# Storing the partial sums of a GLU two rows at a time, with transfer prices and ranks of the order fitted anew

## The chip, the cores and the metric

The kernel runs on one core of one Trainium2 chip. The metric is the time of one execution on the device in microseconds; lower is better. Engines are named as in the profile: PE (TensorE matmul), PEld (its weight load), DVE (VectorE), ACT (ScalarE), POOL (GpSimd) and SP (SyncE, which here only issues transfers).

## The reference

Two branches work on the same input and are mixed row by row. A is a state-space convolution along the sequence, done with Fourier transforms; B is a bilinear GLU without a nonlinearity. A gate of one number per row mixes them.

```python
x = A_u                                                # 1 x 2048 x 512, float32
g = _sigmoid((x * gate_w).sum(-1, keepdims=True))
a = _A_ref(x, log_A_real, A_imag, C_real, C_imag, log_dt, D_skip)   # irfft(rfft(u) * rfft(K)) + u * D_skip
b = einsum((einsum(x, w_gate) * einsum(x, w_up)), w_down)           # F = 1792
return g * a + (1 - g) * b
```

The kernel K of the convolution is itself computed, from 128 complex exponentials for each of 512 channels.

## The kernel before

**GLU.** The 1792 hidden columns are cut into 14 pieces f of 128, in four groups of 3, 3, 4 and 4 (`GROUPS`). The 2048 rows are cut into four column blocks ci of 512, each of four output rows r of 128 partitions, so that an output row t = 4 ci + r is one 128x512 tile, 256 KB. For each group gi and block ci, `hidden(f)` multiplies x by w_gate and w_up into the two PSUM banks pg and pu (one of each), ACT copies pg to h, DVE multiplies pu by h, and h is split into a high part hh (ACT) and a low part hl (DVE). `down` then multiplies by w_down into y (two PSUM banks). Every product is made of three matmuls of 128x512 in fp32r, from the high and low parts of both operands (whi and wlo, xs, dhi and dlo, hh and hl): low times high, high times low, high times high.

**The sums.** `evacuate` (line 722) takes a finished y: ACT scales it by the negated gate into a tile acc, and the tile leaves for the output in memory. In the first group SP stores it; in the others POOL adds it to what is there (`accum_op=ALU.add`). The last block of the last group (`LAST` = 0) is the exception: its four rows stay on the chip and are finished by `ends`, which loads the sums so far and stores the final rows. There are three acc tiles of one row, so the fourth row of a block needs the landing of the first one's transfer.

**Convolution.** Its tables are computed by DVE and ACT for 16 channel blocks, each followed by a matmul step `k_block`; after every fourth come the transforms (`k_first`, `m_second`, `m_inverse`, `m_last`). All their matmuls write tiles named k. They lie between the GLU's matmuls on PE. Intermediate results travel through memory (su_d, sk_d, y_d), and the final pieces are added to the output by POOL.

**The start.** `first_loads` fetches the first x in four pieces of 256 KB (SP) and the first weights w0 in four pieces of 128 KB (the first by ACT's queue, the rest by SP's); `first_split` cuts a piece into high (ACT) and low (DVE), and the first f starts as the pieces come.

**What sets the order.** The program lists all tasks with their engine, an assumed duration, a rank and, for transfers, an assumed size `dma`. `Work.plan` plays the run through with these figures, one task at a time: the one that can start first, ties by rank and place in the list. The order it finds on each engine is what is written out; every engine works strictly in that order. So a changed figure changes the order of the whole run, though not the work. Its figures for transfers: `Bus` serves SP's and POOL's queues side by side with the weights `WEIGHT`; `SENT` and `LANDED` are delays before and behind a transfer; `SURE` is how much later than the planned landing a task that needs the data is placed; `FETCH` and `BEHIND` describe the loading of PE's instructions; `ROOM` says how far an ordinary task may delay an urgent one (h, hh, hl); `EASE` shifts single kinds of tasks by a slack, a rank or a place in the list:

```python
t.slack, t.rank, t.late = t.slack + slack, t.rank + rank, t.late + late
...
if d.dma and d.start > 20.0 and task.engine in self.SURE:
    return d.end + self.SURE[task.engine]
...
for d, end in bus.add(t, start + self.SENT[t.engine], t.dma / self.DMA_RATE / 1000):
    d.end = end + self.LANDED[d.engine]
```

A transfer of figure 256 thus takes 256 / 0.33 / 1000 = 0.78 us in the plan. Instructions are recorded under one line of a helper (L124), so the profile's groups are told apart by the names of the tiles.

## Time and profile before

| | |
|---|---|
| median of three runs | 581.37 us (581.23 to 582.0) |
| the profiled execution's own time | 581.93 us |
| its span, first to last instruction | 580.1 us |
| PE busy | 573.5 us, 99% |
| DVE, ACT, POOL busy | 510.9, 401.6, 113.5 us |
| DMA packets, bytes | 71687, 136.28 MB |

A busy time is the union of an engine's instructions. In the list of groups, a row gives the operation, out<-in with the shapes, the count, busy us, mean ns of one, and the idle time before them with what ended it. In the list of transfers a row gives the issuing queue, the count, KB of each and the median time from issue to landing. The chain of waits follows the run back from its last instruction.

### The profile page before, as it was taken

What the parts mean: (1) busy time and instruction counts of PE and PEld (TensorE: products, weight loads), DVE (VectorE), ACT (ScalarE), POOL (GpSimd) and SP (SyncE); (2) the same over time, 40 slices, a digit from 0 to 9 for tenths busy, and PEclk for the clock granted to TensorE, in tenths of its full rate; (3) what the DMA queues carried; (4) which work ended last, traced back from release to release, by engine and by line L of the source; (5) the groups of instructions that cost most, each with busy time, mean ns of one, the idle gap of its engine ahead of it and who ended that gap; (6) DMA issues with size and microseconds to landing.
All of it is one profiled execution on the core that took longest, in us unless ns stands there. A gap on an engine that the chain in (4) does not pass through costs nothing.

```text
span 580.1 us, 14843 instructions
## 1 busy us (share of the span) xinstructions
PE 573.5 (99%) x5998; PEld 433.8 (75%) x5998; DVE 510.9 (88%) x812; ACT 401.6 (69%) x891; POOL 113.5 (20%) x159
## 2 busy tenths in 40 slices
PE   9999999999999999999999999999999999999997
PEld 6777776888886877788677878876868786776775
DVE  6999999999998999999999999997999996347655
ACT  5459888898588589967896775799877544343351
POOL 0003222311111150321132401102333103111011
PEclk9999999999999999999999999999999999999999
DMA  8999959998655797998779757978989439798986
GB/s 284 403 354 358 395 216 354 269 231 232 140 173 128 281 228 173 261 216 273 201 226 250 188 135 238 213 198 206 292 147 292 72 134 289 246 293 222 291 166 128
DMA packets 71687, 136.28 MB, mean 235 GB/s; under 512 B 6852, under 2 KB 35780, under 8 KB 69188
## 3 DMA queue, kind: packets, MB, share of 16 engines
q1 hardware_dynamic: 47668, 87.10, 43.7%
q0 software_dynamic: 23392, 47.98, 39.6%
q8 instruction: 47, 0.77, 0.6%
q10 hardware_dynamic: 560, 0.26, 0.2%
q14 instruction: 20, 0.16, 0.1%
HBM read 80.27 MB, written 55.05 MB: 233 GB/s over the span
## 4 chain that ended last, share of the span: by engine, by line
PE 97%; DMA 1%; ACT 1%; DVE 1%; issue 0%; DVEq 0%; ACTq 0%
PE pg L124 27%; PE y L124 27%; PE pu L124 27%; PE k L124 16%; DMA y<-in_xT 1%; ACT h L124 0%; DVE y L124 0%; ACT acc L124 0%; ACT xs L124 0%; DVE hl L124 0%; DVE dlo L124 0%; DVE kt L124 0%; DVEq L1568 0%; ACT whi L124 0%; DVE h L124 0%
## 5 line engine op out<-in xcount | busy, mean ns | idle before, releaser
L124 PE MATMUL pg<-xs,whi 128*128 128x512 f32 x448 | 138.9, 391 | 0.4 <-ACT whi L124 0.4
L124 PE MATMUL pu<-xs,whi 128*128 128x512 f32 x448 | 138.2, 390 | 0.0
L124 PEld LDWEIGHTS pg<-xs,whi 128*128 128x128 f32 x448 | 84.3, 188 | 17.7 <-ACT whi L124 0.6
L124 PEld LDWEIGHTS pu<-xs,whi 128*128 128x128 f32 x448 | 84.1, 188 | 17.0
L124 PE MATMUL y<-dhi,hl 128*128 128x512 f32 x224 | 90.2, 403 | 0.7 <-DVE hl L124 0.6
L124 PE MATMUL pg<-xs,wlo 128*128 128x512 f32 x224 | 89.9, 401 | 0.8 <-ACT h L124 0.7
L124 PE MATMUL pu<-xs,wlo 128*128 128x512 f32 x224 | 89.3, 399 | 0.0
L124 PE MATMUL y<-dlo,hh 128*128 128x512 f32 x224 | 87.6, 391 | 0.0
L124 PE MATMUL y<-dhi,hh 128*128 128x512 f32 x224 | 87.1, 389 | 0.0
L124 POOL DMA_DIRECT2D out<-acc x44 | 38.5, 930 | 171.6 <-ACT acc L124 171.0
L124 ACT COPY ev<-k 128x512 f32<-128x512 f32 x112 | 59.3, 597 | 15.8 <-PE k L124 13.3
L124 ACT CAST hh<-h 128x512 fp32r<-128x512 f32 x56 | 34.7, 620 | 41.7 <-DVE h L124 41.3
L124 DVE TENSOR_TENSOR h<-pu,h 128x512 f32<-128x512 f32 x56 | 38.6, 689 | 26.3 <-PE pu L124 23.9
L124 ACT ACTIVATE acc<-y,ngate 128x512 f32<-128x512 f32 x62 | 42.0, 689 | 24.3 <-PE y L124 23.2
L124 PEld LDWEIGHTS pg<-xs,wlo 128*128 128x128 f32 x224 | 42.1, 188 | 21.5 <-issue 10.1
L124 PEld LDWEIGHTS y<-dhi,hl 128*128 128x128 f32 x224 | 42.0, 187 | 21.6 <-issue 8.3
L124 ACT COPY h<-pg 128x512 f32<-128x512 f32 x56 | 33.0, 590 | 32.4 <-PE pg L124 28.6
L124 PEld LDWEIGHTS pu<-xs,wlo 128*128 128x128 f32 x224 | 42.0, 188 | 16.7 <-issue 7.0
L124 PEld LDWEIGHTS y<-dhi,hh 128*128 128x128 f32 x224 | 42.1, 188 | 9.0
L124 PEld LDWEIGHTS y<-dlo,hh 128*128 128x128 f32 x224 | 42.1, 188 | 8.1 <-issue 0.3
L124 DVE TENSOR_TENSOR hl<-h,hh 128x512 fp32r<-128x512 f32 x56 | 38.4, 686 | 3.6 <-ACT hh L124 3.1
L124 DVE TENSOR_TENSOR v<-m,v 128x896 f32<-128x896 f32 x32 | 34.0, 1084 | 0.2
(130 smaller groups left out, 959.1 us busy)
## 6 DMA issues: line engine op xcount, KB each, us to landing
xs<-xs_d SPq DMA_DIRECT2D x36, 512.0 KB, 5.8
out<-acc POOLq DMA_DIRECT2D x44, 256.0 KB, 6.4
raw<-in_wts SPq DMA_DIRECT2D x33, 256.0 KB, 4.9
xs_d<-xs SPq DMA_DIRECT2D x16, 512.0 KB, 6.8
su_d<-ev POOLq DMA_DIRECT2D x32, 256.0 KB, 6.1
y_d<-ts SPq DMA_DIRECT2D x28, 256.0 KB, 6.1
in<-su_d POOLq DMA_DIRECT2D x12, 512.0 KB, 8.0
sk_d<-ev SPq DMA_DIRECT2D x6, 1024.0 KB, 3.9
```

Of the source, the lines that this page charges most:

```text
L124: got = getattr(self.engine, name)(*args, **kw)
```

## The change

1. **Sums in pairs.** A tile acc holds two rows, `[P, 2, D]`, and there are two such tiles instead of three of one row. ACT fills the halves as the two y come; the transfer of both rows starts after the second, with one run of 4 KB for each partition instead of two of 2 KB. There are 8 stores by SP and 22 additions by POOL where there were 16 and 44. The two rows that `ends` takes over lie in the halves of one tile.
2. **A shared buffer.** The convolution's small products and squares (tile `sq`) use the buffer `m` of the large ones.
3. **The first tile.** The first quarter of x comes in two halves of 64 partitions, by SP's and by ACT's queue; the first piece of w0 follows on ACT's queue. The weights of f = 0 are laid out on the host so that each of the four pieces is one run of 1 KB per partition instead of two of 512 B; `product` and `first_split` index them accordingly. The high part of w0's first piece is cast by DVE instead of ACT.
4. **Figures.** The sizes `dma` of most transfers, and `WEIGHT`, `SENT`, `LANDED`, `SURE`, `FETCH`, `BEHIND`, `ROOM`, are set anew, and so is the table `EASE`.

```diff
+PAIR = 620
 class Bus:
-    WEIGHT = 1.0, 1.58
+    WEIGHT = 1.0, 1.24
...
-    BLOCK, FIRST, LEAD, FETCH = 256, 193, 64, 5.0
+    BLOCK, FIRST, LEAD, FETCH = 256, 193, 64, 5.5
-    ROOM = {"dve": 0.6, "act": 0.4}
+    ROOM = {"dve": 0.7, "act": 0.4}
-    BEHIND = 1.3
+    BEHIND = 1.05
     EASE = {
-        "act:k/e:0.4": (3, 0, 0),
+        "act::0.21": (1, 0, 0),
+        "act:k/ev:0.59": (0.0, -1, 0),
+        "act:k/x:0.32": (0.0, -1, 0),
+        "act:k/x:0.59": (0.5, 0, 0),
...
-        "act:t/rt:0.77": (0.0, 0, -200),
-        "act:ts/xs:0.62": (0.0, 2, 0),
-        "dve:ev/y:0.6": (3, 0, 0),
-        "dve:in/whi/wlo:0.69": (0.0, 1, 0),
-        "dve:k/in:0.42": (3, 0, 0),
+        "act:ri/v:1.46": (0.5, 0, 0),
+        "act:v/sq:1.17": (0.0, 0, 20),
+        "act:y/acc:0.69": (0.0, 0, 60),
+        "dve:in/whi/wlo:0.69": (0.0, 1, -200),
+        "dve:k/kt:0.42": (0.0, -1, 0),
...
-        "pe:kt/k/ri/e:2.13": (0.0, 0, -200),
+        "dve:m/v:1.09": (0.0, 0, -20),
+        "dve:v/x:0.4278": (0.0, 0, -200),
+        "sp:in:0.42": (0.0, 1, 0),
+        "sp:raw:0.42": (3, 0, 0),
-    SENT = {"sp": 1.15, "act": 1.15, "pool": 1.98}
-    LANDED = {"sp": 1.79, "act": 1.79, "pool": 1.5}
-    SURE = {"pe": 3, "act": 2, "dve": 2}
+    SENT = {"sp": 1.35, "act": 1.35, "pool": 1.86}
+    LANDED = {"sp": 1.56, "act": 1.56, "pool": 1.62}
+    SURE = {"pe": 3, "act": 1.5, "dve": 1.5}
...
-        add("sp", 0.42, lambda: sp.dma_start(t.t, src), w=[t], dma=256, rank=rank)
+        add("sp", 0.42, lambda: sp.dma_start(t.t, src), w=[t], dma=305, rank=rank)
...
-        add("pool", 0.95, lambda: pool_q.dma_start(lo.t, src, accum_op=ALU.add), w=[lo], dma=485 * n if n > 1 else 414, rank=0)
+        add("pool", 0.95, lambda: pool_q.dma_start(lo.t, src, accum_op=ALU.add), w=[lo], dma=416 * n if n > 1 else 361, rank=0)
...
-            add("sp", 0.42, lambda t=t, k=k, kt=kt: sp.dma_start(t.t[:, k], xsrc(kt)), w=[(t, k)], dma=256, rank=-1)
             e, q = ("sp", sp) if kt else ("act", act)
-            add(e, 0.42, lambda q=q, ks=ks: q.dma_start(w0.t[:, :, ks], wsrc[:, :, ks]), w=[(w0, ("k", kt))], dma=128, rank=-1)
+            cuts = (slice(0, P // 2), slice(P // 2, P)) if kt == 0 else (slice(0, P),)
+            for n, cut in enumerate(cuts):
+                ex, qx = ("act", act) if n else ("sp", sp)
+                add(
+                    ex, 0.42, lambda t=t, k=k, kt=kt, cut=cut, qx=qx: qx.dma_start(t.t[cut, k], xsrc(kt)[cut]),
+                    w=[(t, (k, n)) if len(cuts) > 1 else (t, k)], dma=256 // len(cuts), rank=-1,
+                )
+            add(e, 0.42, lambda q=q, ks=ks: q.dma_start(flat[:, ks], wts[0][:, ks]), w=[(w0, ("k", kt))], dma=128, rank=-1)
...
-        add("act", 0.38, lambda: act.copy(cut(hi.t), src()), r=[(t, k)], w=[(hi, k)], rank=0)
+        if kt:
+            add("act", 0.38, lambda: act.copy(cut(hi.t), src()), r=[(t, k)], w=[(hi, k)], rank=0)
+        else:
+            add("dve", 0.35, lambda: dve.tensor_copy(cut(hi.t), src()), r=[(t, k)], w=[(hi, k)], rank=0)
...
-    def product(pg, which, w, x, kt, after, first):
-        base = which * D + kt * P
+    def product(pg, f, which, x, kt, after, first):
+        w = ws[f]
+        base = which * D + kt * P if f else 2 * kt * P + which * P
...
     def evacuate(gi, ci, r, y):
-        t = 4 * ci + r
+        t, k = 4 * ci + r, r % 2
...
-        acc = new("glu", "acc", [P, D], bufs=3)
+        if not k:
+            sums["acc"] = new("glu", "acc", [P, 2, D], bufs=2)
+        acc = sums["acc"]
         add(
-            "act", 0.69, lambda: act.activation(acc.t, y.t, AF.Copy, scale=ngate[:, t : t + 1]),
-            r=[y, (m_gate, ci)], w=[acc], rank=0,
+            "act", 0.69, lambda: act.activation(acc.t[:, k], y.t, AF.Copy, scale=ngate[:, t : t + 1]),
+            r=[y, (m_gate, ci)], w=[(acc, k)], rank=0,
         )
         if final:
-            ending.append((r, acc))
+            ending.append((r, lambda: acc.t[:, k], (acc, k)))
+        elif not k:
+            return
         elif gi == 0:
-            add("sp", 0.42, lambda: sp.dma_start(ov[:, t, :], acc.t), r=[acc], w=[(m_out, t)], dma=134)
+            add(
+                "sp", 0.42, lambda: sp.dma_start(ov[:, t - 1 : t + 1, :], acc.t), r=[acc],
+                w=[(m_out, t - 1), (m_out, t)], dma=392,
+            )
         else:
             add(
-                "pool", 0.95, lambda: pool_q.dma_start(ov[:, t, :], acc.t, accum_op=ALU.add),
-                r=[acc, (m_out, t)], dma=431, rows=[t],
+                "pool", 0.95, lambda: pool_q.dma_start(ov[:, t - 1 : t + 1, :], acc.t, accum_op=ALU.add),
+                r=[acc, (m_out, t - 1), (m_out, t)], dma=PAIR, rows=[t - 1, t],
             )
...
-        q = new("tab", "sq", [P, 2, 2, TB, 3])
+        q = new("tab", "m", [P, 2, 2, TB, 3])
...
-            sq = new("tab", "sq", [P, TB, 16])
+            sq = new("tab", "m", [P, TB, 16])
...
+    wts[0, :, : 2 * D] = wts[0, :, : 2 * D].reshape(P, 2, KT, P).transpose(0, 2, 1, 3).reshape(P, 2 * D)
```

More of the change, by code (lines that the diff above doesn't have):

```diff
@@ L694, in hidden @@
         for which, kt in pairs:
-            product(pg[which], which, ws[f], x[kt], kt, after, not steps[1:] and f == 0)
+            product(pg[which], f, which, x[kt], kt, after, not steps[1:] and f == 0)
         h = new("glu", "h", [P, D])
@@ L750, in ends @@
         )
-        for r, acc in ending:
+        for r, acc, had in ending:
             t = t0 + r
@@ L767, in total @@
                     dve.scalar_tensor_tensor(
-                        sums.t[:, r, cs], acc.t[:, cs], scale, sums.t[:, r, cs], op0=ALU.mult, op1=ALU.add
+                        sums.t[:, r, cs], acc()[:, cs], scale, sums.t[:, r, cs], op0=ALU.mult, op1=ALU.add
                     )
-                add("dve", 0.42 if r == 3 else 0.69, total, r=[acc, (m_gate, LAST)], w=part, rank=0)
+                add("dve", 0.42 if r == 3 else 0.69, total, r=[had, (m_gate, LAST)], w=part, rank=0)
                 e, q = ("act", act) if n else ("sp", sp)
@@ L1236, in k_first @@
                     ),
-                    r=[st], w=[(m_sk, (q, m)) for m in range(n0, n0 + n, 8)], dma=41 * n,
+                    r=[st], w=[(m_sk, (q, m)) for m in range(n0, n0 + n, 8)], dma=50 * n,
                 )
@@ L1274, in m_load @@
                 ),
-                r=[(m, (q, n0)) for n0 in range(0, 32, 8 if w else 4)], w=[(t, (T, w))], dma=655 if w else 585,
+                r=[(m, (q, n0)) for n0 in range(0, 32, 8 if w else 4)], w=[(t, (T, w))], dma=574 if w else 544,
             )
@@ L1458, in m_last @@
                 lambda rs=rs, flat=flat: pool_q.dma_start(ov[:, rs[0] : rs[-1] + 1, cs], flat(), accum_op=ALU.add),
[L1459 removed]
+                r=[*parts, *((m_out, r) for r in rs)], dma=129 * len(rs), rows=rs,
             )
```

39 lines of the change are left out of this document (18 added, 21 removed).

## The prediction

> **What bounds the kernel now.** I read the page first: busy time of the engines, then the chain that ended last.
>
> ```profile
> span 580.1 us, 14843 instructions
> PE 573.5 (99%) x5998; PEld 433.8 (75%) x5998; DVE 510.9 (88%) x812; ACT 401.6 (69%) x891; POOL 113.5 (20%) x159
> PE 97%; DMA 1%; ACT 1%; DVE 1%; issue 0%; DVEq 0%; ACTq 0%
> ```
>
> TensorE is busy for 99% of the span and makes up 97% of the chain. No other engine sets the end. A change can therefore move the time in three places only: before the first product, in the places where TensorE stands still, and after the last product. The busy time by stretches, cut at the first product and at the end of the last one, gives their sizes.
>
> ```profile
> 0.00:5.62 5.62, 4.21 (x7) 1.85 (x7) 0.65 (x5) 2.21 (x3) 0.96 (x25) 1.00 0.64 177
> 5.62:576.37 570.75, 569.32 (x5992) 431.92 (x5992) 509.37 (x806) 399.39 (x888) 112.51 (x134) 1.00 0.84 236
> 576.37:580.20 3.83, 0.00 (x1) 0.00 (x0) 0.88 (x2) 0.00 (x0) 0.00 (x0) 0.98 0.63 191
> ```
>
> The columns are the stretch, its length, busy time of PE, PEld, DVE, ACT and POOL, the granted clock, the DMA share and GB/s. The head is 5.62 us, the tail 3.8 us, and the clock is full throughout. "PE busy" hides part of a stop, because the modelled ends of matmuls overlap. So I measure stops from start to start. The chain of waits, in order of time, gives the undisturbed rate:
>
> ```profile
> 142.31 2.72 PE y L124 x12
> 145.03 1.92 PE k L124 x128
> 146.95 1.58 PE y L124 x6
> ```
>
> Twelve matmuls of 128x512 take 2.72 us, or 0.227 us each. Six should take 1.36; the six behind a visit to the convolution's k work take 1.58, so each return costs 0.22. Now the places where TensorE came late, from the timeline (start, duration, what, idle before):
>
> ```profile
> 25.33 0.39 PE L124 MATMUL y<-dhi,hh 128*128 128x512 f32 x1
> 26.27 0.50 PE L124 MATMUL y<-dhi,hl 128*128 128x512 f32 x1 [0.56 <-DVE hl L124]
> 26.61 0.39 PE L124 MATMUL y<-dlo,hh 128*128 128x512 f32 x1
> ...
> 420.42 0.61 PE L124 MATMUL pu<-xs,whi 128*128 128x512 f32 x2
> 421.71 0.19 PEld L124 LDWEIGHTS pg<-xs,wlo 128*128 128x128 f32 x1 [1.10 <-ACT h L124]
> 421.71 0.50 PE L124 MATMUL pg<-xs,wlo 128*128 128x512 f32 x1 [0.67 <-ACT h L124]
> 422.04 0.62 PE L124 MATMUL pg<-xs,whi 128*128 128x512 f32 x2
> ...
> 570.63 0.19 PEld L124 LDWEIGHTS y<-dhi,hl 128*128 128x128 f32 x1 [0.52 <-ACT acc L124]
> ```
>
> At 26.27 the matmul was due at 25.33 + 0.227 = 25.56: 0.71 lost, and another 0.11 as its successor starts 0.34 and not 0.23 later: 0.82 us. At 421.71 it was due at 420.42 + 2 x 0.227 = 420.87: 0.84 + 0.11 = 0.95 us. There the weight load shows 1.10 idle for 0.84 lost, so a load's idle time less 0.26, plus 0.11, is the loss. That turns the waits of the weight loads into losses:
>
> ```profile
> PEld pg L124 <- ACT h L124: 2.9, 5, 1.1
> PEld y L124 <- DVE hl L124: 1.0, 1, 1.0
> ```
>
> The five waits for the copy h hold the 1.10 just priced, 0.42 at 11.81 (row below) and three more, (2.9 - 1.10 - 0.42) / 3 = 0.46 each: 0.27 at 11.81, 0.31 each for the three. The wait for acc at 570.63 costs 0.52 - 0.26 + 0.11 = 0.37.
>
> ```profile
> 11.81 0.19 PEld L124 LDWEIGHTS pg<-xs,wlo 128*128 128x128 f32 x1 [0.42 <-ACT h L124]
> ...
> 0.74 0.86 SPq L124 DMA_DIRECT2D y<-in_xT  x2
> 0.74 0.47 ACTq L124 DMA_DIRECT2D ev<-in_wts  x1
> 4.64 0.62 ACT L124 CAST xs<-y 128x512 fp32r<-128x512 f32 x1 [1.60 <-DMA y<-in_xT]
> 5.17 0.40 ACT L124 CAST whi<-ev 128x256 fp32r<-128x256 f32 x1
> 5.29 0.69 DVE L124 TENSOR_TENSOR xs<-y,xs 128x512 fp32r<-128x512 f32 x1 [4.13 <-ACT xs L124]
> 5.62 1.17 PE L124 MATMUL pg<-xs,whi 128*128 128x512 f32 x2 [0.35 <-ACT whi L124]
> 5.90 0.42 DVE L124 TENSOR_TENSOR wlo<-ev,whi 128x256 fp32r<-128x256 f32 x1
> 6.63 0.40 PE L124 MATMUL pg<-xs,wlo 128*128 128x512 f32 x1
> ```
>
> The first product's third matmul starts at 6.63 where 5.62 + 2 x 0.227 = 6.07 was possible: 0.56. All stops: 0.56 + 0.27 + 0.82 + 3 x 0.31 + 0.95 + 0.37 = 3.90 us. This budget, 0.7% of the span, and the head are all that any new order can win back.
>
> **The change part by part.** *Sums in pairs.* The transfers of acc, in the list of DMA issues, beside the nearest relative: an adding transfer of 512 KB, 4 KB to a partition.
>
> ```profile
> out<-acc POOLq DMA_DIRECT2D x44, 256.0 KB, 6.4
> wlo<-in_wts POOLq DMA_DIRECT2D x11, 512.0 KB, 6.8
> out<-acc SPq DMA_DIRECT2D x16, 256.0 KB, 6.3
> raw<-in_wts SPq DMA_DIRECT2D x33, 256.0 KB, 4.9
> ```
>
> On POOL 44 issues become 22, on SP 16 become 8; a pair should land some 6.8 us after its issue instead of 6.4 for a single row. POOL saves 22 issues. One is priced here:
>
> ```profile
> L124 POOL DMA_DIRECT2D out<-acc x44 | 38.5, 930 | 171.6 <-ACT acc L124 171.0
> ```
>
> That is 22 x 0.93 = 20 us of an engine that stood idle for 171 us before these very issues: nothing on the path. The row to leave first now waits for the second, one row's down products later: 9 or 12 matmuls, 2.0 to 2.7 us. Behind the waiting instruction on POOL stand the loads of wlo and dlo and those of the convolution's su_d and sk_d; on SP, in the first group, the raw loads and the copies xs_d. The planner places the pair after its second row, so POOL is held for less than these 2.7 us, against a stock of 171. Two pair tiles give more room than three single ones: a tile is asked for again two pairs later, after the whole hidden part of the next step (three or four f of 2 x 2.72 us, at least 16 us), against a landing of 6.8. With three tiles the fourth row needed the first row's landing, yet among the stops above only the last one, 0.37 us, is behind acc, and its rows are no longer stored by these transfers. I take 0 for the pairs; bounds 0.4 gained (the 570.63 wait) and, where SP or POOL is held by the late row at a load that TensorE then misses, one stop like 421.71, 0.95 lost.
>
> *sq into m.* The table's small products take the buffer of the large ones. DVE's table work already ran in this order (m, the two squares, the next leads), as each step reads its forerunner. Cost 0. If the cover went, one outer product of 1.08 us would wait for a square; TensorE sees it only through a late k visit, and the plan can put k visits elsewhere.
>
> *First tile.* x's first 256 KB go half by SP's and half by ACT's queue, and the first quarter of the first weights, now one 1-KB run per partition, is issued on ACT's queue behind that half: 0.47 us later than before. Its cast moves from ACT (0.40) to DVE, where DVE must then do the cast, xs low and wlow in a row: 0.42 + 0.69 + 0.42 = 1.53, with the cast taken at the price of a DVE operation of that size (0.42). Before, this weight piece landed at the latest at 5.17. If it still lands near 5.0, the third matmul starts at 5.0 + 1.53 + some 0.1 = 6.63: no change. Bounds: it lands as early as the x tile did, 4.64: 0.4 won; it is late by the whole 0.47: 0.5 lost. I take 0: ACT is relieved, DVE gets as much on its chain.
>
> The Trainium skill, "DMA: Bandwidth & Descriptors", section "Issuing engines are not separate DMA queues", says that transfers started from SP and ACT run on the same 16 DMA engines and interleave, and that a second issuer saves issue time alone. By it the half tile gains nothing but the 0.43 of one issue and the weights pay 0.47, so this term would be +0.5 and the sum 580.2 instead of 579.7.
>
> *Refitted prices and ranks.* The raw loads are now planned at 305 instead of 256, the sums at 620 per pair, the weight of POOL's queue falls from 1.58 to 1.24, the margin for work on landed data from 2 to 1.5 us, and the list of nudges is replaced. No instruction is added; the order on all engines is new. Of the 3.90 us of stops some stay in any order: the start (0.56, taken above), 11.81 (one pu product, 3 x 0.227 = 0.68 us, lies between the last pg product and the next, against the copy h of 0.62 and two hand-overs; pg has one bank), and 570.63 (the last rows have nothing between them): 1.20 us. Free to go are 2.70. The largest shows how it arose:
>
> ```profile
> 418.98 0.62 ACT L124 CAST dhi<-raw 128x512 fp32r<-128x512 f32 x1 [0.81 <-DMA raw<-in_wts]
> 419.77 1.46 ACT L124 COPY v<-ri 128x128 f32<-128x128 f32 x4
> 421.04 0.62 ACT L124 COPY h<-pg 128x512 f32<-128x512 f32 x1
> ```
>
> A raw load landed 0.81 us later than planned, ACT stood at it, and h came behind. The raised raw price, (305 - 256) / 0.33 = 148 ns of transfer, aims at just this; the smaller margin takes 0.5 away again. Bounds for the order: all 2.70 gone, or as many new stops of 0.95 as there are misjudged loads. A merged or split k visit moves 0.22, three either way 0.7. I take 1.7 won: the 2.70 go, and one stop the size of the largest (0.95, rounded to 1.0) comes in their stead, as the margin shrinks.
>
> **Sum.** 0 (pairs) + 0 (sq) + 0 (start) - 1.7 (order) = -1.7. The profiled execution took 581.93 us, its span 580.13 and 1.80 around it; the median of the runs, 581.37, lies 0.56 lower. So 581.93 - 1.7 - 0.56 = 579.67 in medians.
>
> **The rivals.** *The stops are only dealt anew.* Every stop that goes is replaced by another. For it: in 570 us only seven stops behind the start, so the old order was well fitted already, and a refit of prices by a tenth cannot be told from chance. Against it: the largest had a cause that the refit names. Time: 581.4.
>
> *Margins too thin (the slower side).* ACT and DVE run in order; with 0.5 us less margin a late cast of raw data stands ahead of h or hl, and TensorE stops as at 421.71. Price 0.95 each; the old stops stay, and two come on top: 581.37 + 1.9 = 583.3. It decides from the second on (0.2% is 1.16 us). For it: a raw landing was 0.81 late even with the margin of 2, and the DMA engines are busy at 0.84. Against it: single landings of the sums no longer compete so much, and raw is priced higher.
>
> *The pieces stay 2 KB.* If the hardware's packets are cut at 2 KB, the DMA relief is missing; then only the new order counts, and I put it at 581.4, as the order was made for a relief that isn't there.
>
> **How the numbers follow.** Forecast 579.7 (own range 578.0 to 580.2): 0.50. Dealt anew: 0.27. Pieces stay 2 KB: 0.03. Too thin: 0.20. What a measurement of this kernel can tell from no change is about 0.2%, 1.16 us: faster is below 580.2, slower above 582.5. So faster 0.50, same 0.30, slower 0.20. Low end of the range: 581.37 - 2.70 - 0.4 (pairs) - 0.4 (start) = 577.9; high end, 583.3 of the slower rival, leaves out a tenth on each side at most.
>
> **What would show it.** Right: PE's matmuls still 0.227 apart, x5998; 22 and 8 issues of out<-acc of 512 KB, POOL's near 6.8 us to landing; POOL busy near 94; the first product's third matmul at 6.2 to 7.1; waits of pg's loads for h below 2.0 us, and none for hl. Wrong: a sum of stops above 4 us, new waits of ACT or DVE for raw, ts or in tiles just ahead of a PE stop, or a chain in which another engine than PE holds more than 4%.

## The result, and the profile after

The changed kernel takes 589.86 us (median of four runs, 589.07 to 590.27), the kernel before 581.68 us (581.23 to 582.29) beside it. By these medians it is 8.2 us slower. The ratio on record is 1.0125, with a 95% interval of 1.0103 to 1.0147; it isn't the quotient of the two medians (1.0141), and the same holds for the ratios below. The forecast was 579.7 us, the range 577.9 to 583.3.

The page of the kernel after: span, busy times, the chain by engine, the group and the transfers of the sums.

```profile
span 588.5 us, 14781 instructions
PE 575.5 (98%) x5998; PEld 434.9 (74%) x5998; DVE 512.3 (87%) x813; ACT 398.8 (68%) x890; POOL 94.1 (16%) x137
DMA packets 66871, 136.28 MB, mean 232 GB/s; under 512 B 6388, under 2 KB 34804, under 8 KB 64372
PE 96%; ACT 1%; issue 1%; DMA 1%; DVE 1%; DVEq 0%; ACTq 0%
L125 POOL DMA_DIRECT2D out<-acc x22 | 19.3, 877 | 174.8 <-ACT acc L125 174.8
out<-acc POOLq DMA_DIRECT2D x22, 512.0 KB, 6.4
```

The sums came out as described: 22 additions of 512 KB, 6.4 us to land, POOL down from 113.5 to 94.1 us, the same bytes in 4816 fewer packets. Nothing there is on the path. TensorE's instructions are the same 5998, and still 96% of the chain, yet the span grew by 8.4 us. So TensorE stood still for longer, or ran slower. Its waits (total us, times, longest):

```profile
PE pg L125 <- DVE whi L125: 3.1, 1, 3.1
PE k L125 <- issue: 2.5, 2, 1.7
PE k L125 <- ACT h L125: 1.6, 1, 1.6
PE k L125 <- DVE acc L125: 1.1, 1, 1.1
PE y L125 <- DVE hl L125: 0.6, 1, 0.6
PE pu L125 <- issue: 0.4, 1, 0.4
```

They are few and long; the one of 1.1 us lies ahead of the warm-up and was there before, as was the one of 0.6. Measured from start to start, as in the prediction, the 8.37 us of span (588.50 - 580.13) divide thus:

- **The start, 3.24 us.** The second weight pair's first matmul starts at 15.05 us instead of 11.81.
- **Stops behind it, 5.08 us** (7.78 in all against 2.70). Kept are 0.72, 0.21, 0.21 and 0.26. Gone are 0.84 at 421.71 and three of 0.10 to 0.20. New are 1.96 in the visit to the convolution's work at 130.65, 0.56 at 263.97, 1.56 at 362.29, 1.63 at 439.02, 0.41 at 455.42, and 0.12 and 0.14.
- The rest, 0.05: one visit more (61 for 60, some 0.2 for the return) against a tail shorter by 0.1.

**The start in the timeline of after** (start, duration, engine, what, idle before and what ended it):

```profile
4.89 1.28 ACT L125 ACT_TABLE_LOAD   x1 [4.89 <-DMA y<-in_xT]
6.18 1.14 ACT L125 CAST xs<-y 128x512 fp32r<-128x512 f32 x2
6.83 0.69 DVE L125 TENSOR_TENSOR xs<-y,xs 128x512 fp32r<-128x512 f32 x1 [5.67 <-ACT xs L125]
7.44 0.29 DVE L125 CAST whi<-ev 128x256 fp32r<-128x256 f32 x1
7.87 1.19 PE L125 MATMUL pg<-xs,whi 128*128 128x512 f32 x2 [3.08 <-DVE whi L125]
8.86 0.63 PE L125 MATMUL pg<-xs,wlo 128*128 128x512 f32 x1
```

and the same row of ACT in the timeline of before:

```profile
1.75 1.28 ACT L124 ACT_TABLE_LOAD   x1 [1.75 <-issue]
```

The first product comes 2.25 us later (7.87 for 5.62), in three parts. x's first tile lands 0.25 later (4.89 for 4.64). The load of ACT's function table, which ran at 1.75 us in idle time, now stands behind this landing: 1.28. The cast now waits for two landings, one of each half, and in the trace one of these waits sits on the table load ahead of it. Then the weights' cast on DVE queues behind xs low: from ACT's first cast to the product it is 1.69 us instead of 0.98, 0.71 more. The remaining 0.99 us are lost within the first eight products: they take 7.18 us to the second weight pair where 6.19 did. The windows of after show why (stretch, length, busy PE, PEld, DVE, ACT, POOL, granted clock, DMA share, GB/s):

```profile
7.00:8.00 1.00, 0.13 (x1) 0.16 (x1) 0.97 (x3) 1.00 (x3) 0.00 (x0) 0.80 1.11 266
8.00:9.00 1.00, 1.00 (x3) 0.81 (x4) 1.00 (x3) 1.00 (x4) 0.00 (x0) 0.50 0.98 365
11.00:12.00 1.00, 1.00 (x6) 0.83 (x5) 0.97 (x6) 0.38 (x1) 0.00 (x0) 1.00 0.99 397
```

TensorE idled from 4.79 to 7.87, the granted clock fell to one half (by the trace's records from 7.60 to 11.01), and matmuls start 0.427 us apart instead of 0.227 until about 11.

**The stops named "issue"** in the timeline of after, two of them:

```profile
130.65 1.98 PE L125 MATMUL k<-v,x 128*32 128x64 f32 x124
134.30 0.31 PE L125 MATMUL k<-v,x 128*32 128x64 f32 x4 [1.67 <-issue]
...
362.29 0.61 PE L125 MATMUL k<-in,w2s 32*32 32x512 f32 x1
363.73 1.25 PE L125 MATMUL k<-in,w2s 32*32 32x512 f32 x31 [0.83 <-issue]
```

They break into the middle of a visit, after 124 of its 128 matmuls and after 1 of 32, and no engine releases them. Counted over all instructions that the trace has for TensorE (matmuls, weight loads and its own waiting instructions), it resumes behind 1729 of them at 134.30, behind 4801 at 263.97 and behind 7105 at 363.73. All are 193 + 256 n: the places at which a block of 256 instructions ends. The queue that brings such blocks shows it in the transfers of 131.5 to 133 us:

```profile
q8 instruction: 1, 0.02, 4.1%
```

This block came from 131.89 to 132.87 us; TensorE had run out at 132.4 and resumed 1.43 us after the block's end. The others resumed 1.43 and 1.41 us after theirs (the last block ended at 362.32, TensorE resumed at 363.73). The short stop at 455.42 is put down to the same: matmuls go on at 455.87, 1.46 us after the end of a block, within 13 instructions of 9153 = 193 + 256 x 35; closer the trace's order of weight loads and matmuls can't be counted there. The planner knows of these blocks (`BLOCK`, `FIRST`, `LEAD`): it takes a block as asked for 320 instructions ahead of its first one and as there `FETCH` + `BEHIND` times the load later. In the trace, 11.7, 7.1 and 9.6 us passed between the two. A visit of the kind k_block issues 256 instructions in 2 us, a whole block, where GLU products take 29 us for as many; after such a visit the next block can be late.

**The stop at 439.02**, put down to ACT's h, in POOL's and PE's timelines of after and the transfers of 425 to 440 us:

```profile
429.62 1.58 POOL L125 DMA_DIRECT2D out<-ts  x1 [5.90 <-ACT hh L125]
431.39 0.91 POOL L125 DMA_DIRECT2D in<-sk_d  x1 [0.18 <-issue]
439.02 1.15 PE L125 MATMUL k<-in,w2s 32*32 32x512 f32 x32 [1.55 <-ACT h L125]
```

```profile
in<-sk_d POOLq DMA_DIRECT2D x1, 512.0 KB, 7.5
```

The read of sk_d left POOL at 431.39 behind out<-ts and landed 7.5 us later, at 438.9. The visit started there; it waited for this landing, not for h.

### The profile page after: what moved, and what is told of

Read it like the earlier page. It is cut to its first block, busy times and chain, and to the rows that moved or that the text cites. A ratio compares the mean times of both kernels' runs of the same rounds, so it can differ in the third digit from the quotient of the medians.

```text
span 588.5 us, 14781 instructions
## 1 busy us (share of the span) xinstructions
PE 575.5 (98%) x5998; PEld 434.9 (74%) x5998; DVE 512.3 (87%) x813; ACT 398.8 (68%) x890; POOL 94.1 (16%) x137
## 4 chain that ended last, share of the span: by engine, by line
PE 96%; ACT 1%; issue 1%; DMA 1%; DVE 1%; DVEq 0%; ACTq 0%
PE pg L125 26%; PE pu L125 26%; PE y L125 26%; PE k L125 17%; DMA y<-in_xT 1%; ACT ev L125 0%; ACT h L125 0%; DVE y L125 0%; ACT L125 0%; ACT acc L125 0%; DVE xs L125 0%; ACT xs L125 0%; DVE hl L125 0%; ACT hh L125 0%; ACT v L125 0%
## 5 line engine op out<-in xcount | busy, mean ns | idle before, releaser
L125 POOL DMA_DIRECT2D out<-acc x22 | 19.3, 877 | 174.8 <-ACT acc L125 174.8
L125 PEld LDWEIGHTS k<-v,x 128*32 128x32 f32 x2048 | 29.6, 110 | 7.5 <-issue 5.7
```

What stands on the lines that cost most here:

```text
L125: got = getattr(self.engine, name)(*args, **kw)
```

## The experiments

Two theories stood at first. One: the loss is in single places (start, late blocks, one landing) and each can be won back. The other: what is won in one place is handed on to a later one. Then came a third question: does the loss belong to the change's parts or to the order that the planner made with them?

### The start

*The table load early*: a copy of one column, in ACT's idle time ahead of the first landing.

```diff
+    add("act", 0.2, lambda: act.copy(ngate[:, 0:1], shift), r=[m_const], w=[m_gate], rank=0)
```

> The changed kernel with one tiny ACT copy ahead of the first cast; the order of all else is the changed kernel's. In the changed kernel the load of ACT's tables stands at 4.89 us, behind the landing of one half of the first tile, and takes 1.28; before, it stood at 1.75 in idle time. Theory T (the half tile makes the first cast wait for two landings, and the table load in front of it takes one of these waits): the table load goes back to 2 to 3.5 us, the first cast from 6.18 to about 4.9, the first product from 7.87 to about 6.6, and with the shorter stop of TensorE less of the 50% clock: 1.3 to 2.6 us faster than the changed kernel, 587.3 to 588.6. Rival D (the halves simply arrive late through two queues): the cast stays after 5.5, under 0.7 us gained.

589.24 us (ratio 1.0105, 1.0069 to 1.0142). The table load ran at 2.55, the first cast at 4.45, the first product at 6.15 instead of 7.87, but the second weight pair came at 13.81, 1.24 earlier only, since the matmuls still started 0.427 us apart. Here that isn't the effect of a stop: the trace's clock records begin only at 10.32 us, with the full clock, and there the matmuls become fast; in the kernel after, the full clock is on record from 4.18. The clock had not yet come up. (The windows list 1.00 where there is no record.) Behind the start stood stops of 1.85, 1.57, 1.52 and 1.97 us at block ends and at 439. The time hardly moved.

*Table early, and DVE's cast ahead of xs low.*

```diff
+    add("act", 0.2, lambda: act.copy(ngate[:, 0:1], shift), r=[m_const], w=[m_gate], rank=0)
...
-        for t in self.plan():
+        order = self.plan()
+        order.remove(self.cast)
+        order.insert(next(n for n, t in enumerate(order) if t.engine == "dve" and t.us == 0.69), self.cast)
+        for t in order:
             t.fn()
```

> As the one before, and the first weight cast on DVE ahead of the low part of x, behind which it stood in the changed kernel. Theory T: the weights landed at 5.04 (1.34 + 3.7), so the cast is done at 5.4, xs by 5.5; first product near 5.6 instead of 7.87, no slow clock, the whole 3.24 us of the start back: about 586.6. Rival D: no more than 1.5 us back.

588.21 us (1.0104, 1.0041 to 1.0166; the single runs lay between 585.2 and 593.6). The first matmul came at 5.71, but its xs low was now late; matmuls again 0.427 us apart up to the first clock record at 10.43, the second weight pair at 13.80.

*The start of before within the order of after*: x's first tile whole by SP, the weights' first cast on ACT.

```diff
+        def whole(t, k, kt, cut, qx):
+            if qx is sp:
+                sp.dma_start(t.t[:, k], xsrc(kt))
...
-                    ex, 0.42, lambda t=t, k=k, kt=kt, cut=cut, qx=qx: qx.dma_start(t.t[cut, k], xsrc(kt)[cut]),
+                    ex, 0.42, lambda t=t, k=k, kt=kt, cut=cut, qx=qx: whole(t, k, kt, cut, qx),
...
-            add("dve", 0.35, lambda: dve.tensor_copy(cut(hi.t), src()), r=[(t, k)], w=[(hi, k)], rank=0)
+            work.cast = add("dve", 0.35, lambda: act.copy(cut(hi.t), src()), r=[(t, k)], w=[(hi, k)], rank=0)
```

> The start of the kernel before (first tile whole by SP, first weights first on ACT's queue, their cast on ACT) inside the order of the changed kernel; only the host layout of the first weights stays changed. If the start is 3.24 us of the loss: first product at 5.6 and 586.6 in all, the other 5 us of loss stay. If the loss at the start is due to the other order behind it, under 1 us comes back.

590.91 us (1.013, 1.0095 to 1.0164). The second weight pair came at 12.10, so 2.95 us of the start were won, and all of it was given back: 2.21 us and seven matmuls at 0.427 after a late block in the visit at 127.6, 2.67 in the one at 388.4, 1.60 ahead of 440.7. So the loss at the start comes from the split first tile and the DVE cast; that the total falls by as much, as expected, is not so.

*The block figures of before.*

```diff
-    BLOCK, FIRST, LEAD, FETCH = 256, 193, 64, 5.5
+    BLOCK, FIRST, LEAD, FETCH = 256, 193, 64, 5.0
-    BEHIND = 1.05
+    BEHIND = 1.3
```

> The changed kernel with FETCH and BEHIND of before (5.0 and 1.3 instead of 5.5 and 1.05): only the plan's idea of how late a block of PE's instructions can be under DMA load. Theory F (the stops of TensorE without a releaser, at 134.3, 264.0, 363.7 and 455.9, are missing instruction blocks, which the lower BEHIND lets the plan run into): three or four of the four stops, together 4.5 us, vanish, and new ones of the kind are rare: 585 to 587. Rival C (any new order deals such stops by chance): the sum of stops without a releaser stays within 2 us of 4.5.

588.3 us (1.0116, 1.0073 to 1.0159). A new order, with no stop at 263, 439 or 455, but 1.91 at 129.6, 1.61 at 360.3, 0.84 at 427.7. Of these the first two are late blocks (TensorE resumes at 133.15 and 361.79, 1.2 and 1.5 us after a block's end), and a third, 0.5, comes at 355.65: some 4 us by late blocks as before, the rival's side. The refit of these two figures isn't the cause by itself.

### The parts, one and two at a time

Each was undone or done alone, and the planner made its order anew. *Pairs and the shared buffer alone, in the kernel before*:

```diff
+        if not k:
+            sums["acc"] = new("glu", "acc", [P, 2, D], bufs=2)
...
-        q = new("tab", "sq", [P, 2, 2, TB, 3])
+        q = new("tab", "m", [P, 2, 2, TB, 3])
```

> The kernel before with the sums in pairs (4-KB pieces, two tiles of two rows, planned at 620 and 392) and the shared buffer m, nothing else: start, figures and nudges as before. Theory P (the pairs cost nothing, they lie beside PE's work, and the figures' margin for instruction blocks, 5.0 and 1.3, still guards the order): at most one stop behind a missing instruction block, 580.5 to 583.5. Rival C (any new order draws such stops): two or more of them, over 584.

*Start and figures, without the pairs* (the changed kernel with the two hunks above taken back):

```diff
-            sums["acc"] = new("glu", "acc", [P, 2, D], bufs=2)
+        acc = new("glu", "acc", [P, D], bufs=3)
```

> The changed kernel with the sums by single rows again and their old prices (134 and 431); start, other figures and nudges as changed. If the pairs are the cause of the stops behind instruction blocks: these vanish and only the start's 3.2 us is left, about 585. If the start and the refitted figures are: start lost as in the changed kernel, two or more block stops, 587 to 591.

*The figures alone* (pairs and start taken back):

```diff
-            sums["acc"] = new("glu", "acc", [P, 2, D], bufs=2)
+        acc = new("glu", "acc", [P, D], bufs=3)
...
-                    ex, 0.42, lambda t=t, k=k, kt=kt, cut=cut, qx=qx: qx.dma_start(t.t[cut, k], xsrc(kt)[cut]),
+            add("sp", 0.42, lambda t=t, k=k, kt=kt: sp.dma_start(t.t[:, k], xsrc(kt)), w=[(t, k)], dma=256, rank=-1)
```

> The kernel before with the new figures and nudges alone (sums by single rows, old start). Theory F (the refit lets k work stand where PE's next instruction block has not come): first product at 5.6, but two to four stops at instruction numbers 193 + 256 n, 583.5 to 587. If the refit is harmless by itself: no such stop over 0.5 us, 580 to 583.

*Pairs and start, with the figures and nudges of before*:

```diff
-    WEIGHT = 1.0, 1.24
+    WEIGHT = 1.0, 1.58
...
-    SURE = {"pe": 3, "act": 1.5, "dve": 1.5}
+    SURE = {"pe": 3, "act": 2, "dve": 2}
```

> The kernel before with the new start and the pairs, with the figures and nudges of before. Theory T + F: first product at 6.6 to 7.9 after a table load that waits for a half tile, first matmul of the second f some 2 to 3.3 us later than the 11.81 of before, no more than one block stop: 583.5 to 586. If the loss is all in the refitted order: under 582.5.

*Pairs and figures, without the start*:

```diff
-            add("dve", 0.35, lambda: dve.tensor_copy(cut(hi.t), src()), r=[(t, k)], w=[(hi, k)], rank=0)
+        add("act", 0.38, lambda: act.copy(cut(hi.t), src()), r=[(t, k)], w=[(hi, k)], rank=0)
```

> The changed kernel without the start's part (first tile's transfers, weights' layout, the cast on VectorE undone), planned anew. Theory: each combination is a new order with its own late blocks and its own end, so that nothing adds up: 585 to 597 us. Rival: the start is the loss of 3.24 us and the rest is as in the changed kernel: 586.6.

| parts | us | ratio | from TensorE's last start to the end |
|---|---|---|---|
| pairs | 592.59 | 1.0175 (1.0148 to 1.0203) | 14.8 |
| start, figures | 598.53 | 1.0272 (1.0237 to 1.0307) | 11.4 |
| figures | 596.75 | 1.0230 (1.0185 to 1.0275) | 11.8 |
| pairs, start | 588.27 | 1.0105 (1.0072 to 1.0139) | 6.7 |
| pairs, figures | 588.04 | 1.0109 (1.0071 to 1.0147) | 4.1 |
| all three | 589.86 | 1.0125 (1.0103 to 1.0147) | 4.1 |

The pairs alone and the figures alone cost more than all together (the start alone wasn't run). The second, third and fourth came out above both times that were expected of them; the first lies on its rival's side, but without the late blocks that the rival called for; only the last, pairs and figures, lies in its theory's range, a wide one. With the pairs alone TensorE starts its last matmul at 575.98, as before, but the convolution's last visit moves from 563.60 to 574.62 us, in the timeline of that kernel:

```profile
574.62 1.95 PE L125 MATMUL k<-x,w_t 64*32 64x512 f32 x32
```

What follows it then has no GLU work beside it, and this longer end alone makes up the 10.6 us by which the span grew. The table suggests that two chains, the GLU on TensorE and the convolution over DVE, ACT and the transfers, have to end together, and that figures and nudges fitted to one set of parts no longer see to that for another; no run isolates this. So nothing is added up from these runs, and the start isn't the whole loss: without it the kernel is at 588.04.

### The late blocks

*The block ends 24 instructions sooner, in the kernel before.* The warm-up's three matmuls become nine, 36 instructions for 12; order and work stay.

```diff
-            for n in (4, 4, 1):
+            for n in (1,) * 9:
```

> The kernel before with its warm-up of three matmuls of 512, 512 and 128 columns cut into nine of 128: 36 TensorE instructions in place of 12, so that every later block of 256 ends 24 instructions sooner in the program. Order and work are the same. Theory (late blocks): the visits that used to end just within a block now meet its end while the next block is still on its way; by the time from instruction 193 + 256 n - 320 to the block's end in the trace of before, less 6.9 to 8.4 us for fetch and start, stops without a releaser of 0.5 to 2.0 us come at 229 us and at 339 us, 2.1 to 3.6 us at 536 us, and less at 226 and 263 us; the time rises by 3 to 8 us to 585 to 590. Rival (the stops are of another kind): the time stays within 0.5 us of 582.

587.15 us (1.0078, 1.0063 to 1.0093), 4.8 more than before. The stops came at instructions 4033 and 7873 of this kernel, again 193 + 256 n; in the kernel before they lie elsewhere in the work. One is the expected one (229 us, 0.97), the other was not on the list (379 us, 3.1); 339 and 536 stayed free. The timeline at 379 and the windows behind it:

```profile
379.25 1.99 PE L124 MATMUL k<-v,x 128*32 128x64 f32 x128
384.27 0.80 PE L124 MATMUL pg<-xs,wlo 128*128 128x512 f32 x1 [3.03 <-issue]
```

```profile
380.00:382.00 2.00, 1.24 (x91) 1.08 (x79) 1.97 (x4) 2.00 (x10) 0.00 (x0) 1.00 1.06 213
382.00:384.00 2.00, 0.00 (x0) 0.00 (x0) 1.78 (x2) 0.74 (x1) 0.86 (x1) 0.86 1.00 277
384.00:386.00 2.00, 1.73 (x4) 1.44 (x5) 0.00 (x0) 0.00 (x0) 0.00 (x0) 0.50 0.92 177
```

Behind the stop the granted clock is 0.50, and 14 matmuls start late, nearly all by 0.20 us: 2.9 us on top of the stop itself. The stop of 0.84 us at 421.71 went. Here only the place of the block ends was changed (the second weight pair came at 11.78 for 11.81), so the cause is shown. How late a block is, is not told by its place alone: this one began to come 10.0 us after instruction 7873 - 320, where the block of the kernel before near there took 6.7.

*Three visits behind further products of the GLU*, in the changed kernel. `LATER` gives the TensorE instruction at which the visit lies and the number of products that go ahead of it; what needs the visit moves with it.

```diff
+    LATER = {1600: 4, 4600: 2, 6900: 3}
...
+            order[i - len(moved) - len(kept) + 1 : i + 1] = kept + moved
```

> The changed kernel with three convolution visits of 256 TensorE instructions moved later in the order, behind 4, 2 and 3 further products of the GLU: the ones that end in the stops of 1.96 us at 132.4, 0.56 us at 263.2 and 1.56 us at 362.3. Theory: these stops are instruction blocks of 256 that arrive late, since a visit uses a whole block up in 2 us; with 2.7, 1.4 and 2.0 us of products ahead of the block's end they vanish, TensorE passes there without a stop of over 0.2 us, and the time falls by up to 4.1 us, to 585.8. Rival: the stop belongs to the visit itself (its operands, or what follows it); then it travels with the visit, stays as long, and the time stays 589.9. A third: the time is taken back by other stops later, as it was when the start alone was won back; then these three are gone and the sum of the others grows by as much.

588.27 us (1.0104, 1.0061 to 1.0146; single runs 584.8 to 592.0). The stop of 1.96 is gone. The one at 263 grew, in this kernel's timeline:

```profile
260.53 1.98 PE L125 MATMUL k<-v,x 128*32 128x64 f32 x124
264.50 0.41 PE L125 MATMUL k<-v,x 128*32 128x64 f32 x4 [1.99 <-issue]
```

It is still at instruction 4801, not at the visit's old place, so the rival falls; but its block came only at 262.97, and seven matmuls behind it were slow. The third move had no effect, 1.74 us, and rightly: the whole visit still lay within the 320 instructions ahead of the block's end, and the time for them was 8.1 us as against 8.2. The total hardly moved.

*Longer warm-up*, the changed kernel with TensorE kept busy until the first operands come.

```diff
-            for n in (4, 4, 1):
+            for n in (4, 4, 4, 4):
```

> The changed kernel with a longer warm-up: 4, 4, 4, 4 groups of 128 columns instead of 4, 4, 1, so that TensorE, which stood idle from 4.79 to 7.87 us, is busy until about 7.7. All else and its order stay. Theory: the first products start 0.427 us apart instead of 0.227 because TensorE idled before them; then they come 0.227 apart, the second weight pair's first matmul moves from 15.05 to about 13.65 us, and the time is 588.4 (less whatever a later stop takes back). Rival: the distance comes from operands that arrive late (DVE's and ACT's casts); then it stays 0.427, that matmul stays at 15.05 and the time at 589.9.

587.6 us (1.0115, 1.0086 to 1.0143). The windows of this kernel:

```profile
8.00:9.00 1.00, 1.00 (x6) 0.79 (x6) 1.00 (x4) 0.00 (x0) 0.00 (x0) 1.00 0.86 267
```

Six matmuls in a microsecond for three, the clock full: from the first product to the second weight pair 5.92 us for 7.18. The idle time was the cause of the slow ones. The first product also came sooner (6.59), as the half of x's first tile that the table load waits for had landed by 3.60; over the runs this landing lay between 3.60 and 4.89 us, and why isn't settled. The blocks at 128 and 361 us were late again, by 2.37 and 1.25.

*Start of before and six visits moved.*

```diff
+    LATER = {1600: 4, 3800: 2, 4600: 2, 6900: 3, 7700: 4, 8650: 3}
```

> The changed kernel with the first tile loaded and cast as in the kernel before, and six convolution visits behind 2 to 4 further products of the GLU: the three above, the ones near 231 and 388 us, and the one at 439.02 that waited for a landing. Theory: what the changed kernel lost is the start (2.95 us by the run that restored it), the late blocks (4.1 us) and the late landing (1.6 us), and the three add: 589.9 - 8.65 = 581.2, no slower than the kernel before. Rival: time won ahead is handed on to the next late block or landing, as when the start alone was restored; then over half of it comes back and the time is 586 or more.

587.71 us (1.0089, 1.0069 to 1.011): the rival's side. The second weight pair came at 12.71. Stops at 128, 231, 263 and 388 are gone; 1.63 at 358 and 1.37 at 438 remain, and a visit moved later made its follower late (1.38 at 394.64).

*Longer warm-up and four visits moved.*

```diff
-            for n in (4, 4, 1):
+            for n in (4, 4, 4, 4):
...
+    LATER = {1600: 4, 4600: 4, 7100: 3, 9100: 2}
```

> The changed kernel with the longer warm-up (4, 4, 4, 4 groups) and four convolution visits moved later: the one near 128 us and the one near 260 us behind 4 further products each, the second of the two near 361 us behind 3, the one near 452 us behind 2. Theory: the stops of 2.37 and 0.56 us vanish, 1.25 us falls to about 0.5 (only 8 of this visit's instructions lay ahead of the block's end, so that 3 products add 0.75 us), 0.48 vanishes; the span falls from 584.8 to about 580.7 and the time from 587.6 to 583.5. Rival (time won is handed on): the span stays over 583.

587.12 us (1.0083, 1.0064 to 1.0102), again the rival. Gone at 128; 1.66 at 360; and at 436.5 the landing of sk_d was late by 2.5 us, with eight slow matmuls behind.

### Another order from the same parts

*The kernel before, one figure of one kind of transfer 1% off.*

```diff
-                    add("sp", 0.42, lambda t=t, g=g, half=half: halves(q, t, g, half), r=y_parts(q, half), w=[(t, half)], dma=512)
+                    add("sp", 0.42, lambda t=t, g=g, half=half: halves(q, t, g, half), r=y_parts(q, half), w=[(t, half)], dma=517)
```

> The kernel before with one planning figure of one kind of transfer changed by 1%, 512 to 517 KB for the reads of y; the transfers themselves and all work stay, but the planner makes another order from about half of the program on. Theory A (the order of before is a selected one, and nearly any new order loses by late blocks and landings): 584 to 592 us. Theory B (the loss of the changed kernel belongs to its parts): 581.7 as before, within 1 us.

582.51 us for 582.35 (1.0004, 0.9996 to 1.0013), with no new stop over 0.4 us. A new order doesn't lose as such; theory A falls for this kernel.

*The changed kernel, one figure 1% off.*

```diff
-            add(e, 0.42, lambda q=q, ks=ks: q.dma_start(flat[:, ks], wts[0][:, ks]), w=[(w0, ("k", kt))], dma=128, rank=-1)
+            add(e, 0.42, lambda q=q, ks=ks: q.dma_start(flat[:, ks], wts[0][:, ks]), w=[(w0, ("k", kt))], dma=129, rank=-1)
```

> The changed kernel with one planning figure changed by 1%, 128 to 129 KB for the pieces of the first weight tile; all work stays, the planner makes another order. Theory A (a new order deals new stops, with nothing of the change in them): a time between 582 and 593 us, the stops without a releaser at other places than in the changed kernel. Theory B (the loss belongs to the parts, whatever the order): 589.9 within 1 us.

582.85 us for 582.35 (1.0004, 0.999 to 1.0019): 7 us less than the changed kernel, for the same work and the same transfers. Its span, busy times and all waits of TensorE:

```profile
span 582.5 us, 14772 instructions
PE 574.6 (99%) x5998; PEld 434.3 (75%) x5998; DVE 511.5 (88%) x813; ACT 399.4 (69%) x890; POOL 94.2 (16%) x137
```

```profile
PE pg L125 <- DVE whi L125: 2.5, 1, 2.5
PE k L125 <- DVE acc L125: 1.1, 1, 1.1
PE y L125 <- DVE hl L125: 0.6, 1, 0.6
```

The start is as in the changed kernel (second weight pair at 15.04); no wait for "issue" is left, and the stops behind the start sum to 1.69 us, 1.01 less than before. Two more runs ask whether this order and a mended start add. *This order, with the longer warm-up*:

```diff
-            for n in (4, 4, 1):
+            for n in (4, 4, 4, 4):
```

> The changed kernel with 129 for 128 in that one planning figure, and the longer warm-up (4, 4, 4, 4 groups). Theory (order and start are separate losses and add): the start comes back as it did in the changed kernel's own order (12.51 for 15.05 us at the second weight pair's first matmul), no stop without a releaser appears, and the time falls by 2.5 us from 582.85 to 580.3. Rival (in this stage time won ahead is handed on to late blocks): stops of 1 to 3 us appear at 128 to 440 us and the time stays at 582 or more.

582.08 us beside 582.16 (1.0000, 0.9990 to 1.0009). Span 580.7, second weight pair at 13.11, stops 1.73: the 1.9 us won at the start stayed won in the profiled execution. The median didn't follow: the ratio to the kernel before went from 1.0004 to 1.0000, some 0.2 us, against 2.5 expected. The profile of the run before had caught one of its longer executions (584.32 in a range of 580.92 to 584.54), so the spans make the gain look larger than the medians do. *Also the table load early, and a warm-up of 4, 4, 4, 1*:

```diff
+    add("act", 0.2, lambda: act.copy(ngate[:, 0:1], shift), r=[m_const], w=[m_gate], rank=0)
-            for n in (4, 4, 1):
+            for n in (4, 4, 4, 1):
```

> As the one before, with 4, 4, 4, 1 groups, and the activation table loaded in the idle time ahead of the first landing (by a copy of one column). Theory: the first cast no longer waits 1.28 us for the table, the first product comes at about 5.7 to 6.1 us, the second weight pair's first matmul at about 11.5 us, and the time falls by 3.5 us to 579.3. Rival: as before, handed on to late blocks: 582 or more. A third: the products then wait for VectorE's casts, as they did when the table alone was moved, and the start stays at 12.5 to 13.8 us: 580.3 to 581.6.

581.35 us beside 582.16 (0.9989, 0.9974 to 1.0003). The timeline of its start:

```profile
2.73 1.28 ACT L125 ACT_TABLE_LOAD   x1 [2.73 <-issue]
4.75 1.29 ACT L125 CAST xs<-y 128x512 fp32r<-128x512 f32 x2 [0.54 <-DMA y<-in_xT]
6.45 0.70 PE L125 MATMUL pg<-xs,whi 128*128 128x512 f32 x2
```

The table is out of the way and the second weight pair comes at 12.49, 2.55 sooner than in the changed kernel; DVE's cast still holds the product to 6.45, as the third case had it. Span 579.4, stops 1.41. Theory and sum agree in direction; the time is the lowest of all versions, but the interval holds 1, so no version is shown to beat the kernel before. The first theory's 579.3 wasn't reached; the third case's 580.3 to 581.6 was.

## Why the prediction was wrong

**Pairs, 0: right.** Issues, landing time and POOL's busy time are as forecast (94.1 for "near 94"; 6.4 us to land for 6.8), and no TensorE wait came from them. The rival "pieces stay 2 KB" falls: the adding queue's packets went from 23392 to 20224.

**sq into m, 0: right** as far as the traces show; no wait of TensorE leads back to it.

**First tile, 0 with bounds -0.4 to +0.5: wrong, it was +3.24.** This is the step that failed for certain. It priced the chain by DVE's three operations and the landing; xs low and the cast do queue as it said, but it left out the table load, which an added wait pulled from idle time onto the path (1.28), took the order cast, xs low, wlow where DVE does xs low first (0.71), and took the full clock for granted behind a longer idle time (0.99). Only the landing, 0.25 later, was within its bounds; it varies by more than that from run to run. The sign that the prediction named for this term, the third matmul at 6.2 to 7.1, failed too: it came at 8.86. By the rule that the prediction took from the Trainium skill, "DMA: Bandwidth & Descriptors", section "Issuing engines are not separate DMA queues", the term would have been +0.5: the right sign and a sixth of the size. That the split brought no earlier landing agrees with that rule: where the table load was out of the way, the first cast had its whole tile at 4.45, 4.75 and 5.04 us; with the tile whole, at 4.49 to 5.04.

**Refitted order, -1.7: wrong, +5.1.** The working priced stops by late casts and hand-overs alone, on the budget of stops that the old trace showed. Late instruction blocks weren't in that trace as stops, and so weren't in the bounds. They were close: the blocks at instructions 1217 and 4801 had ended 1.4 us before their use, no more than TensorE takes to resume behind a late one. The new stops are 6.4 us: 4.5 by late blocks (1.96 + 0.56 + 1.56 + 0.41), 1.6 by the landing at 439, 0.3 small ones; 1.3 us of old stops went. The largest old stop, at 421.71, did go, as forecast. But the term has no fixed value: the same parts with one figure 1% off give -1.0 (stops of 1.69 us for 2.70), on the forecast's side, while another neighbour, with two block figures of before, stayed at 588.3 us. So the step that failed here is the pricing of a new order by the stops of the old one alone; that 7 of the 8 us belong to this order and not to the work is shown by the first neighbour; why the planner came to it is not.

**The rivals.** "Margins too thin" had the sign and called for two stops; the place was another. It was to come from raw data behind the margin `SURE`, and no such stop is among the new ones. "Dealt anew" describes the mechanism best, but its price, nothing on balance, was 5 us off: a deal can be worse than the one that was kept.

**What to look for** was well chosen in one point: the sum of stops above 4 us.

What stays open: why the figures of the change lead to just this order when a neighbour avoids it, how long a block takes under a given load (7.1 to 11.7 us in one run), and whether other starts could gain more than the last run's. The repairs of single stops by hand didn't settle the total: each time, other blocks or landings were late.

## What to carry to other kernels

Where a planner writes out one order, a change to its figures is worth what that one order is worth: compare it with neighbours (a figure 1% off) before the change's parts are credited or blamed. At a kernel's start, check what an added wait is attached to, and what TensorE does meanwhile: here a table load and an idle array cost more than the transfer that was to be sped up. And a stop "issue" inside a row of small matmuls is to be counted in instructions: at a fixed distance from multiples of 256 it is a late block, which no data dependence explains.

## What was unexpected of the hardware

- **Instruction blocks.** TensorE stops at instruction 193 + 256 n when 16 KB of program come late, and resumes 1.2 to 1.6 us after the block's end, in 36 such stops of 15 kernels. The Trainium skill, "Runtime: NRT & Kernel Launch", section "Instruction fetch mechanics", gives the blocks of 256 instructions and calls the cost of crossing one mostly hidden; here it was up to 3.1 us where a visit uses a block up in 2 us beside full transfers.
- **The clock after short stops.** The granted clock is read from records in the trace. In each trace all changes between full and half clock lie whole multiples of 3.41 us apart; a stretch at half clock lasted 3.41 us, once 6.83 (383.46 to 390.29, in the kernel with sooner block ends). All twelve that lie ahead of a run's end followed a stretch of 3.41 us on this grid in which TensorE had stood idle for 54 to 82% of the time, between matmuls. Of the stretches at full clock, none with 47% or less had this effect, and one with 55% (pairs and start) didn't either. So it counts how a stop falls on the grid: 1.99 us inside one stretch halved the clock (264.50, three visits moved), 2.40 us spread over two, 36 and 34%, did not (392.79, start of before). The Trainium skill, "TensorE: Matmul & The Clock Gate", section "What's actually happening", tells of a free-running window of about 3.4 us; the records agree with that window, but a stop well short of a whole one was enough.
- **The table load** takes one of the waits of the instruction behind it once that has two: in all nine kernels with the split tile and no earlier copy on ACT it waited for a landing (3.60 to 4.89 us), in none of the eight with the tile whole (1.66 to 1.76). That moved 1.28 us from idle time onto the path.
- **Scatter.** The order of after, with a mended start, ran between 585.2 and 593.6 us in four runs, the kernel before between 581.0 and 585.2 in all its runs. With the same order behind the start, the block at instruction 1729 was late by 1.9 us in one trace (table early) and not at all in another (table early and cast ahead), so which blocks are late seems to differ from execution to execution; with one trace for each kernel that isn't shown.
